# Which DMA engines carry the first 16 KB of wq's rows in a decode block

## The chip, the cores and the metric

The kernel runs on one core of a Trainium2 chip. The core has five compute engines: TensorE (PE, with its weight loads as PEld), VectorE (DVE), ScalarE (ACT), GpSimd (POOL) and SyncE (SP), and sixteen DMA engines, numbered 0 to 15, that move data between device memory and the on-chip buffer. The metric is the time of one execution in microseconds. The kernel before takes 1314.82 us, the median of three runs (1314.66 to 1314.83).

## The reference

One step of a decoding transformer block in float32, for two sequences of one token each. `x` is 2 x 1 x 512, the key and value caches are 2 x 8 x 32768 x 128 (268 MB each), `wq` is 512 x 4096, `wo` 4096 x 512, the three MLP matrices 512 x 1792, 512 x 1792 and 1792 x 512.

```python
def _A_ref(x, k_cache, v_cache, wq, wo):
    q = (x @ wq) as [B, Hq, Sq, Dh]               # 32 query heads of 128
    k, v = k_cache, v_cache, each head repeated 4 times
    p = softmax(q . k * Dh ** -0.5)               # over 32768 cached positions
    return (p . v as [B, Sq, Hq * Dh]) @ wo

def _B_ref(x, W_gate, W_up, W_down):
    gate = x @ W_gate
    gate = gate * (gate > 0)
    return (gate * (x @ W_up)) @ W_down

xn = _layernorm(x)
return x + _A_ref(xn, ...) * silu(_B_ref(xn, ...))
```

Nearly all of the bytes are the caches, and each is read once.

## The kernel before

**Ring.** All large operands pass through a ring of three slots of 128 partitions x 64 KB (`ring`, `slot`). The first three tiles are `wq`, then the two up-projections of the MLP side by side (`gu`), then the down-projection (`wd`). After them come the caches in groups: for each of the 16 pairs of sequence and key head, two K tiles and two V tiles of 8 MB (`load_k`, `load_v`), and last `wo` in six pieces (`WO_PIECES`). A slot is taken again when the last instruction that reads it is done; so the load of a K or V tile waits on SP, at `L72` (`load`), for the engine that frees the slot three tiles back. The instructions of each engine stand in the order in which the code is written; no scheduler moves them.

**A tile's load.** `wq` is viewed as 128 rows of 64 KB, one to a partition: row p holds matrix rows 4p to 4p+3, 16 KB each. A load over 128 partitions is split evenly over the sixteen DMA engines, eight rows each.

**The moved part of wq.** The first 6 KB of each of the 128 rows (`SHIFT = 1536` values) is left out of the large load and is fetched by loads of its own into a spare part of the third slot (`moved`): six of 20 rows, written with the source as five by four rows, one of five rows and one of three. They stand on SP behind the large `wq` load, with the gate matrix between the fifth and the sixth.

**The projection.** `project_q` multiplies the normalised x (`xnp`, transposed to partitions) with the large part of `wq`, then with the moved rows (`xnx` holds the x values that belong to them, zero where the spare part has no row), all into the same accumulators. The result is turned into `qz`, which the scores use. The MLP (`mlp_gu`, `mlp_h`, `mlp_down`) follows.

**A group.** K is transposed in place by DVE (`turn`, `L355`, the costliest group of instructions), PE forms the scores (`score`, `L369`), ACT the exponentials (`L412`), PE the sum over V (`values`, `L436`). The K tile's slot is free after its scores, the V tile's after its products.

**The end.** The last `wo` piece lands, eight small matmuls (`L536`), two DVE operations (`L566`, `L567`) and the store (`L570`) follow.

Of the kernel before, what the change touches and what calls it, by code (L numbers as in the profile page):

```python
# [13 lines left out]
P = 128  # L14
# [8 lines left out]
SHIFT = 1536  # L23
SPREAD = 5
# [5 lines left out]
def kernel(  # L30
# [37 lines left out]
    def slot(name):  # L68
        return ring.tile([P, SLOT], F32, tag="r", align_bytes=ALIGN, name=name)

    def load(dst, src):
        nc.sync.dma_start(dst, src)  # L72

    wqs, gus, wds = slot("wq"), slot("gu"), slot("wd")
    QN = wq.shape[1]
    HP = P // 2
    SET = 4 * SPREAD
    FULL = P // SET
    REST = [(FULL * SET, SPREAD), (FULL * SET + SPREAD, P - FULL * SET - SPREAD)]
    NT = FULL // 2 + 1  # L80
    load(wqs[:, : SLOT - SHIFT], wq.rearrange("(p i) n -> p (i n)", p=P)[:, SHIFT:])
    moved = wds[:HP, FI * D : FI * D + NT * SHIFT].rearrange("p (t n) -> p t n", t=NT)

# [7 lines left out]
    nc.gpsimd.memset(moved, 0.0)
# [7 lines left out]

    first_rows = wq.rearrange("(p i) n -> p i n", i=NKC)[:, 0, :SHIFT]  # L100

    def place_of(k):
        return slice(Q * (k % 2), Q * (k % 2) + SET), k // 2

    for k in range(FULL + len(REST)):
        if k == 5:
            load_gu(0, wg)
        part, t = place_of(k)
        if k < FULL:
            rows = first_rows[k * SET : (k + 1) * SET, :]  # L110
            load(moved[part, t, :], rows.rearrange("(b a) n -> a b n", b=4))
        else:
            at, n = REST[k - FULL]
            dst = moved[part, t, :].rearrange("(a b) n -> a b n", b=4)[:n, 0, :]
            load(dst, first_rows[at : at + n, :])
# [7 lines left out]
    nc.gpsimd.memset(eps_t, EPS)  # L123
    HQR = Q // NS
# [17 lines left out]
    nc.vector.memset(o_ps, 0.0)  # L142

# [13 lines left out]
    xnx = const.tile([HP, NT, 32], F32, name="xnx")  # L157
    nc.vector.memset(sq, 0.0)
    xfirst = xc.rearrange("m (p i) -> m i p", i=NKC)[:, 0, :]
    for k in range(FULL + len(REST)):  # L160
        to = sq[:, k * Q : k * Q + SET].rearrange("m (a b) -> m a b", b=4)
        if k < FULL:
            cols = xfirst[:, k * SET : (k + 1) * SET]
            nc.vector.tensor_copy(to, cols.rearrange("m (b a) -> m a b", b=4))
        else:
            at, n = REST[k - FULL]
            nc.vector.tensor_copy(to[:, :n, 0], xfirst[:, at : at + n])
# [3 lines left out]
    for t in range(NT):  # L171
        nc.tensor.transpose(
            m_ps[:HP, (NKC + t) * 32 : (NKC + t + 1) * 32],
            sq[:, t * HP : (t + 1) * HP],
            ident[:32, :32],
        )
    nc.vector.tensor_copy(xnp.rearrange("p k m -> p (k m)"), m_ps[:, : NKC * 32])
    nc.vector.tensor_copy(
        xnx.rearrange("p k m -> p (k m)"), m_ps[:HP, NKC * 32 : (NKC + NT) * 32]
    )  # L180

    spread = work.tile([P, 4, 4, Q], F32, tag="row", name="spread", bufs=3)
    for kb in range(4):
        nc.gpsimd.tensor_copy(
            spread[:, :, kb, :], ident.rearrange("p (e l) -> p e l", e=4)
        )
# [35 lines left out]
    def project_q():  # L222
        pick = ident.rearrange("p (c m) -> p c m", c=4)[:, :, :B]
        nq = 2 * REP * 4 * B
        def products(half, part):
            pq = S[0][:, half]
            for k in part:
                for c in range(4):
                    n0 = (half * 4 + c) * 512
                    cut = min(512, max(0, SHIFT - n0))  # L230
                    last = NKC + NT - 1 if cut else NKC - 1
                    i = NKC - 1 - k
                    at = cut if i == 0 else 0
                    if k < NKC and at < 512:
                        lo = i * QN + n0 - SHIFT
                        lhs, rhs, a, b = xnp[:, i, :], wqs[:, lo + at : lo + 512], at, 512
                    elif k >= NKC and cut:
                        t = k - NKC
                        lhs, rhs, a, b = xnx[:, t, :], moved[:, t, n0 : n0 + cut], 0, cut
                    else:  # L240
                        continue
                    nc.tensor.matmul(  # L242
                        pq[32 * c : 32 * c + 32, a:b],
                        lhs,
                        rhs,
                        start=(k == 0),
                        stop=(k == last),
                    )
# [219 lines left out]
    project_q()  # L468
    mlp_gu(0)
    mlp_gu(1)  # L470
    ht = mlp_h()
    mlp_down(ht)

    def load_k(g, u):
        KT[g * NU + u] = load_tile(kc, g * NU + u, f"k_{g}_{u}")
# [128 lines left out]
```

## Time and profile before

| | |
|---|---|
| median of the runs | 1314.82 us |
| the profiled execution's own time | 1314.66 us |
| its span, first to last instruction | 1312.9 us |
| around the span | 1.76 us |
| PE busy | 689.7 us (53%) |
| DVE busy | 638.3 us (49%) |
| ACT, POOL busy | 27.6 us, 11.0 us |
| read from device memory | 564.67 MB, 430 GB/s over the span |
| mean granted TensorE clock | 0.746 |

The times of the page are those of one profiled execution. PE and DVE are each busy half of the time. The row "DMA" in the page's forty slices stands at 9, which means 90% or more, in all but the last slice. A view that gives the busy time of each engine by stretches of the span has at its end the DMA engines' busy share and the rate in GB/s; a share of 1.00 is sixteen engines at work all the time. The list of DMA queues names the packets that come from the kernel's loads (`hardware_dynamic`) and those that fetch instructions (`instruction`).

### The profile page before, as it was taken

Reading aid. Unit: us, or ns where it says so; the run is one execution under the profiler, and the core shown is the slowest. Engines: PE = TensorE matmul, PEld = TensorE weight load, DVE = VectorE, ACT = ScalarE, POOL = GpSimd, SP = SyncE. Lnnn points to the kernel's source line nnn. Section 1 sums busy time; section 2 is a strip of 40 time slices with the busy share of each in tenths; the row PEclk is TensorE's granted clock in tenths of the full one; section 3 lists DMA queues with packets and bytes.
Section 4 is the critical chain, followed back from the end, with each engine's and each line's share of the span. In section 5 each row is a group of like instructions: output and inputs, shape, how many; then the busy total and the mean of one; then the engine's idle time right before and its main releaser. Section 6 shows DMA issues by size and latency. Waiting matters only on the chain.

```text
span 1312.9 us, 9882 instructions
## 1 busy us (share of the span) xinstructions
PE 689.7 (53%) x4614; PEld 184.4 (14%) x4614; DVE 638.3 (49%) x244; ACT 27.6 (2%) x69; POOL 11.0 (1%) x24
## 2 busy tenths in 40 slices
PE   3626266372635637264563726556272654825476
PEld 1201011010111101010120101111010111201121
DVE  2273461916447191653709255281835628178510
ACT  0000000000000000000000000000000000000000
POOL 3000000000000000000000000000000000000000
PEclk9757687785777777677786667877676777867878
DMA  9999999999999999999999999999999999999998
GB/s 406 440 431 438 438 429 430 437 424 443 434 430 438 430 432 438 433 434 436 426 438 432 438 433 434 427 441 424 439 438 428 438 432 430 438 435 428 440 422 342
DMA packets 11059, 565.30 MB, mean 431 GB/s; under 512 B 1281, under 2 KB 1289, under 8 KB 1803
## 3 DMA queue, kind: packets, MB, share of 16 engines
q1 hardware_dynamic: 10974, 564.67, 99.4%
q8 instruction: 36, 0.59, 0.2%
q14 instruction: 5, 0.03, 0.0%
q10 hardware_dynamic: 44, 0.01, 0.0%
HBM read 564.67 MB, written 0.00 MB: 430 GB/s over the span
## 4 chain that ended last, share of the span: by engine, by line
DMA 49%; DVE 25%; PE 24%; issue 1%; ACT 1%; DVEq 0%; ACTq 0%
DMA k<-in_A_k_cache_dram 40%; DVE k L355 21%; PE o_ps L436 10%; PE s L369 7%; PE pt_ps L415 4%; DMA v<-in_A_v_cache_dram 3%; DMA wo<-in_A_wo_dram 3%; DVE pt L419 2%; DMA wq<-in_A_wq_dram 2%; DVE m L379 1%; DMA wd<-in_A_wq_dram 1%; PE m_ps L423 1%; PE s L290 1%; ACT w L412 1%; PE m_ps L404 0%
## 5 line engine op out<-in xcount | busy, mean ns | idle before, releaser
L355 DVE STREAM_TRANSPOSE k<-k 128x8192 f32<-128x8192 f32 (+2 forms) x52 | 553.3, 10666 | 176.4 <-DMA k<-in_A_k_cache_dram 176.4
L369 PE MATMUL s<-k,qz 128*32 128x512 f32 x2048 | 299.1, 742 | 496.5 <-DVE k L355 496.5
L436 PE MATMUL o_ps<-v,pt 128*16 128x512 f32 x2048 | 257.0, 665 | 6.8 <-DMA v<-in_A_v_cache_dram 6.8
L369 PEld LDWEIGHTS s<-k,qz 128*32 128x32 f32 x2048 | 71.0, 132 | 718.8 <-DVE k L355 536.0
L448 DVE SCALAR_TENSOR_TENSOR os<-o_ps,rl,mask 128x512 f32<-128x512 f32 x16 | 12.0, 751 | 252.4 <-PE o_ps L436 252.4
L436 PEld LDWEIGHTS o_ps<-v,pt 128*16 128x16 f32 x2048 | 58.6, 105 | 191.2 <-issue 182.4
L415 PE MATMUL pt_ps<-w,perm 128*128 128x512 f32 x64 | 57.6, 997 | 34.5 <-ACT w L412 17.9
L379 DVE TENSOR_REDUCE m<-s 128x1 f32<-128x1024 f32 x16 | 19.6, 1225 | 89.5 <-PE s L369 89.5
L419 DVE STREAM_TRANSPOSE pt<-pt_ps 128x512 f32<-128x512 f32 x32 | 22.9, 715 | 71.6 <-PE pt_ps L415 71.6
L412 ACT ACTIVATE w<-s,nb 128x512 f32<-128x512 f32 x32 | 21.7, 683 | 1178.6 <-DVE nb L408 1178.6
L415 PEld LDWEIGHTS pt_ps<-w,perm 128*128 128x128 f32 x64 | 14.2, 277 | 54.1 <-issue 36.0
L460 PE MATMUL ot_ps<-os,place 128*128 128x256 f32 x64 | 16.0, 392 | 7.1 <-DVE os L448 7.1
L423 PE MATMUL m_ps<-l,same 128*128 128x1 f32 x32 | 9.4, 362 | 13.5 <-DVE l L422 13.5
L395 PE MATMUL m_ps<-ident,m 128*1 128x128 f32 x16 | 4.3, 270 | 20.4 <-DVE m L379 20.4
L460 PEld LDWEIGHTS ot_ps<-os,place 128*128 128x128 f32 x64 | 11.5, 189 | 15.7 <-DVE os L448 14.4
L423 PEld LDWEIGHTS m_ps<-l,same 128*128 128x128 f32 x32 | 8.0, 311 | 38.7 <-DVE l L422 38.7
L404 PE MATMUL m_ps<-negs,mrow 1*128 1x1 f32 x32 | 6.3, 263 | 10.4 <-DVE mrow L403 10.4
L242 PE MATMUL s<-wq,xnp 128*32 128x512 f32 x58 | 9.0, 739 | 4.5 <-DMA wq<-in_A_wq_dram 4.5
L255 DVE COPY qs<-s 128x512 f32<-128x512 f32 x2 | 1.3, 687 | 19.8 <-PE s L242 19.8
L290 PE MATMUL s<-gu,xnp 128*32 128x448 f32 x64 | 8.6, 692 | 0.8 <-DVE gu L298 0.8
L170 PE MATMUL m_ps<-ident,xc 32*128 32x32 f32 x4 | 0.7, 300 | 14.8 <-DVE xc L155 14.8
L427 DVE RECIPROCAL rl<-m_ps 128x1 f32<-128x1 f32 x16 | 2.7, 169 | 10.8 <-PE m_ps L423 10.8
(78 smaller groups left out, 95.7 us busy)
## 6 DMA issues: line engine op xcount, KB each, us to landing
v<-in_A_v_cache_dram SPq DMA_DIRECT2D x2, 4096.0 KB
wq<-in_A_wq_dram SPq DMA_DIRECT2D x1, 7424.0 KB
wo<-in_A_wo_dram SPq DMA_DIRECT2D x1, 4096.0 KB
gu<-in_B_W_gate_dram SPq DMA_DIRECT2D x1, 3584.0 KB
gu<-in_B_W_up_dram SPq DMA_DIRECT2D x1, 3584.0 KB
wd<-in_B_W_down_dram SPq DMA_DIRECT2D x1, 3584.0 KB
wo<-in_A_wo_dram SPq DMA_DIRECT2D x1, 2048.0 KB
wo<-in_A_wo_dram SPq DMA_DIRECT2D x1, 1024.0 KB
```

The source lines that it names most:

```text
L242: nc.tensor.matmul(pq[32 * c : 32 * c + 32, a:b], lhs, rhs, start=(k == 0), stop=(k == last),)
L290: nc.tensor.matmul(ps[32 * c : 32 * c + 32, :FC], xnp[:, i, :], gut[:, w, i, c * FC : (c + 1) * FC], start=(i == 0), stop=(i == NKC - 1),)
L355: nc.vector.transpose(KT[t][:, part], KT[t][:, part])
L369: nc.tensor.matmul(S[g % 2][Q * c : Q * c + Q, u], qz[:, lo : lo + Q], mov[:, s, c, e], start=(s == 0 and e == 0), stop=(s == NS - 1 and e ...
L379: nc.vector.tensor_reduce(MX[g], S[g % 2], axis=AX.XY, op=ALU.max)
L412: nc.scalar.activation(w, S[g % 2][:, u], AF.Exp, bias=nb, scale=SCALE, accum_out=LS[g][:, u : u + 1])
L415: nc.tensor.matmul(pt_ps, perm, w, start=True, stop=True)
L419: nc.vector.transpose(pt.rearrange("p j m -> p (j m)"), pt_ps)
L423: nc.tensor.matmul(m_ps[:, 300:301], same.rearrange("p r h -> p (r h)"), l, start=True, stop=True)
L436: nc.tensor.matmul(o_ps[Q * a : Q * a + NC * REP], w[:, j, s * NC * REP : (s + 1) * NC * REP], v[:, s, j], start=(u == 0 and s == 0 and j ...
L448: nc.vector.scalar_tensor_tensor(OS[hk][:, b], o_ps, RL.pop(g), mask.unsqueeze(2).to_broadcast([P, NC, DH]), op0=ALU.mult, op1=ALU.mult,)
L460: nc.tensor.matmul(ot_ps.rearrange("p b c i -> p (b c) i"), place[:, lo : lo + P], src[:, dq], start=(hk == 0 and dq == 0), stop=(hk == HK ...
```

## The change

1. `wq` is split elsewhere. Of 80 of the 128 rows, rows 0 to 79, the first 16 KB (one whole matrix row) are left out of the large load; the other 48 rows are loaded whole. The large part is now two loads: 80 rows of 48 KB and 48 rows of 64 KB. Each spreads evenly over sixteen engines, five rows and three rows to an engine.
2. 56 of the 80 pieces of 16 KB are fetched on SP by four loads: 20 rows and 20 rows (five engines, four rows each), 10 rows (five engines, two each) and 6 rows (three engines, two each).
3. The other 24 pieces are fetched by one load that GpSimd issues, as two by twelve rows, which the words of the change give to engines 7 and 8. Ahead of it GpSimd issues a tiny load of seven rows of 32 bytes into a tile that nothing reads (`aside`); the words of the change are that it steps over seven engines.
4. The part of `wq`'s slot that the 80 pieces would have filled is set to zero by GpSimd, so that the products run over the whole slot; the products are all 512 columns wide, 32 of them over the slot and 16 over the moved rows, where there were 29 and 12.
5. The order at the start is turned round: gate, up and down matrices are loaded first, the MLP is computed first, and `wq` comes last. The first K tile is loaded in two halves. Its first half is transposed ahead of the second part of `project_q`.

The bytes that each engine carries of `wq`, in KB, worked out from the shapes of the loads, with the engines that the words of the change name:

| engines | before | after | difference |
|---|---|---|---|
| 0, 1, 2 | 464 + 156 = 620 | 432 + 192 = 624 | +4 |
| 3, 4 | 464 + 150 = 614 | 432 + 160 = 592 | -22 |
| 7, 8 | 464 | 432 + 192 = 624 | +160 |
| 5, 6, 9 to 15 | 464 | 432 | -32 |

The order of the instructions shows three places. The first is SP at the start of the program, whose rows are the loads of the three slots and of the first tiles of the caches. Before:

```order
L72 DMA wq<-in_A_wq_dram 128x14848
L72 DMA wd<-in_A_wq_dram 20x1x1536 x5
L72 DMA gu<-in_B_W_gate_dram 128x7168
L72 DMA wd<-in_A_wq_dram 20x1x1536
L72 DMA wd<-in_A_wq_dram 5x1536
L72 DMA wd<-in_A_wq_dram 3x1536
L72 DMA gu<-in_B_W_up_dram 128x7168
L72 DMA wd<-in_B_W_down_dram 128x7168
L72 DMA k_0_296<-in_A_k_cache_dram 128x16384
L72 DMA k_1_298<-in_A_k_cache_dram 128x16384
```

The same place of the changed kernel:

```order
L72 DMA gu<-in_B_W_gate_dram 128x7168
L72 DMA gu<-in_B_W_up_dram 128x7168
L72 DMA wd<-in_B_W_down_dram 128x7168
L72 DMA wd<-in_A_wq_dram 20x1x4096 x2
L72 DMA wd<-in_A_wq_dram 10x1x4096
L72 DMA wd<-in_A_wq_dram 6x1x4096
L72 DMA wq<-in_A_wq_dram 80x12288
L72 DMA wq<-in_A_wq_dram 48x16384
L72 DMA k_0_253<-in_A_k_cache_dram 128x8192 x2
L72 DMA k_1_304<-in_A_k_cache_dram 128x16384
```

The large part of `wq` went from the first place to the last before the caches, the moved rows stand ahead of it, and the first K tile now takes the slot of `gu`, the second that of `wq`.

The second place is GpSimd near its start, in the changed kernel (`aside` is the tile that nothing reads, `wd` the third slot with its spare part):

```order
L87 MEMSET wd 128x4096
masks.py:197 MEMSET ident 128x128
masks.py:199 ISA
masks.py:199 AFFINE_SELECT ident<-ident 128x128
L116 MEMSET eps_t 32x1
L120 DMA aside<-in_A_x_dram 7x2x4
L102 DMA wd<-in_A_wq_dram 24x1x4096
L125 MEMSET wq 80x4096
L128 MEMSET qz 128x2064
```

Between `eps_t` and `qz` there was nothing before; the two loads and the clearing of `wq`'s slot are new there.

The third place is DVE between the MLP and the first scores, in the changed kernel (`qs`, `turned` and `qz` are the steps that turn the projection into what the scores use):

```order
L318 COPY down<-m_ps 128x512
L349 STREAM_TRANSPOSE k_0_253<-k_0_253 128x8192
L249 COPY qs_278<-s_108 128x512
L249 COPY qs_284<-s_108 128x512
L260 COPY turned<-m_ps 128x64
L273 COPY qz<-pt_ps 32x32x4 x8
```

Before, the copies of `qs`, `turned` and `qz` stood ahead of the MLP's operations, and the whole K tile was transposed in one instruction behind `down`; now half a K tile is transposed between them.

The diff, with the parts left out that only rename:

```diff
-SHIFT = 1536
-SPREAD = 5
+MOVES = ((5, 4, 0, 0), (5, 4, 32, 0), (5, 2, 0, 1), (3, 2, 32, 1), (2, 12, 52, 0))
+UNDER = 7
...
-    load(wqs[:, : SLOT - SHIFT], wq.rearrange("(p i) n -> p (i n)", p=P)[:, SHIFT:])
-    moved = wds[:HP, FI * D : FI * D + NT * SHIFT].rearrange("p (t n) -> p t n", t=NT)
+    OUT = firsts[-1]
+    moved = wds[:, FI * D : FI * D + NT * QN].rearrange("p (t n) -> p t n", t=NT)
...
-    nc.gpsimd.memset(moved, 0.0)
+    nc.gpsimd.memset(moved[:, 0], 0.0)
+    nc.vector.memset(moved[:, 1:], 0.0)
...
-    for k in range(FULL + len(REST)):
-        if k == 5:
-            load_gu(0, wg)
-        part, t = place_of(k)
-        if k < FULL:
-            rows = first_rows[k * SET : (k + 1) * SET, :]
-            load(moved[part, t, :], rows.rearrange("(b a) n -> a b n", b=4))
...
+    def move(k, start):
+        a, b, lo, t = MOVES[k]
+        rows = wqrows[firsts[k] : firsts[k + 1], :QN].rearrange("(b a) n -> a b n", b=b)
+        start(moved[lo : lo + a * b, t, :], rows)
+
+    load_gu(0, wg)
     load_gu(1, wu)
     load(wds[:, : FI * D], wd.rearrange("(p i) d -> p (i d)", p=P))
+    for k in range(len(MOVES) - 1):
+        move(k, load)
+    load(wqs[:OUT, QN:], wqrows[:OUT, QN:])
+    load(wqs[OUT:, :], wqrows[OUT:, :])
...
+    view = x[0, 0, : UNDER * 32].rearrange("(p w) -> p w", p=UNDER)[:, :16]
+    nc.gpsimd.dma_start(
+        aside[:UNDER].rearrange("p (u n) -> p u n", u=2),
+        view.rearrange("p (u n) -> p u n", u=2)[:, :, :4],
+    )
+    move(len(MOVES) - 1, nc.gpsimd.dma_start)
+    nc.gpsimd.memset(wqs[:OUT, :QN], 0.0)
...
-        for part in (range(NKC), range(NKC, NKC + NT)):
-            for half in range(2):
-                products(half, part)
+        for half in range(2):
+            products(half, range(NKC))
+        yield
+        spread = work.tile([P, 4, 4, Q], F32, tag="row", name="spread", bufs=3)
...
+        for half in range(2):
+            products(half, range(NKC, NKC + NT))
...
-    project_q()
-    mlp_gu(0)
-    mlp_gu(1)
-    ht = mlp_h()
-    mlp_down(ht)
...
+    mlp_gu(0)
+    mlp_gu(1)
+    mlp_down(mlp_h())
+    steps = project_q()
+    next(steps)
+    load_k(0, 0, NS)
+    turn(0, 0)
+    for _ in steps:
+        pass
+
     for g in range(NG - 2):
-        for u in range(NU):
+        for u in range(1 if g == 0 else 0, NU):
             load_k(g, u)
```

More of the change, by code (lines that the diff above doesn't have):

```diff
@@ L72, in load @@
         nc.sync.dma_start(dst, src)
-    wqs, gus, wds = slot("wq"), slot("gu"), slot("wd")
+    gus, wqs, wds = slot("gu"), slot("wq"), slot("wd")
     QN = wq.shape[1]
[L76 to L80, printed above, removed]
-    load(wqs[:, : SLOT - SHIFT], wq.rearrange("(p i) n -> p (i n)", p=P)[:, SHIFT:])
-    moved = wds[:HP, FI * D : FI * D + NT * SHIFT].rearrange("p (t n) -> p t n", t=NT)
+    NT = 1 + max(t for *_, t in MOVES)
+    firsts = [sum(a * b for a, b, *_ in MOVES[:k]) for k in range(len(MOVES) + 1)]
+    OUT = firsts[-1]
+    moved = wds[:, FI * D : FI * D + NT * QN].rearrange("p (t n) -> p t n", t=NT)
     row = work.tile([P, 512], F32, tag="row", name="xp", bufs=3)
@@ L98, in load_gu @@
         )
-    first_rows = wq.rearrange("(p i) n -> p i n", i=NKC)[:, 0, :SHIFT]
-    def place_of(k):
-        return slice(Q * (k % 2), Q * (k % 2) + SET), k // 2
-    for k in range(FULL + len(REST)):
-        if k == 5:
-            load_gu(0, wg)
-        part, t = place_of(k)
-        if k < FULL:
-            rows = first_rows[k * SET : (k + 1) * SET, :]
-            load(moved[part, t, :], rows.rearrange("(b a) n -> a b n", b=4))
[L112 to L115, printed above, removed]
+    wqrows = wq.rearrange("(p i) n -> p (i n)", p=P)
+    def move(k, start):
[3 more added lines that the diff above has]
+    load_gu(0, wg)
     load_gu(1, wu)
     load(wds[:, : FI * D], wd.rearrange("(p i) d -> p (i d)", p=P))
+    for k in range(len(MOVES) - 1):
+        move(k, load)
+    load(wqs[:OUT, QN:], wqrows[:OUT, QN:])
+    load(wqs[OUT:, :], wqrows[OUT:, :])
     wdt = wds[:, : FI * D].rearrange("p (i d) -> p i d", i=FI)
@@ L123 @@
     nc.gpsimd.memset(eps_t, EPS)
+    aside = const.tile([P, 8], F32, name="aside")
+    view = x[0, 0, : UNDER * 32].rearrange("(p w) -> p w", p=UNDER)[:, :16]
[5 more added lines that the diff above has]
+    nc.gpsimd.memset(wqs[:OUT, :QN], 0.0)
     HQR = Q // NS
@@ L142 @@
     nc.vector.memset(o_ps, 0.0)
+    nc.vector.memset(xy, 0.0)
     st = const.tile([32, 8], F32, name="st")
@@ L156 @@
     xnp = const.tile([P, NKC, 32], F32, name="xnp")
-    xnx = const.tile([HP, NT, 32], F32, name="xnx")
+    xnx = const.tile([P, NT, 32], F32, name="xnx")
     nc.vector.memset(sq, 0.0)
     xfirst = xc.rearrange("m (p i) -> m i p", i=NKC)[:, 0, :]
[L160 to L167, printed above, removed]
+    sqt = sq[:, : NT * P].rearrange("m (t p) -> m t p", t=NT)
+    for k, (a, b, lo, t) in enumerate(MOVES):
+        nc.vector.tensor_copy(
+            sqt[:, t, lo : lo + a * b].rearrange("m (a b) -> m a b", b=b),
+            xfirst[:, firsts[k] : firsts[k + 1]].rearrange("m (b a) -> m a b", b=b),
+        )
     xcol = xc.rearrange("b (p i) -> b i p", i=NKC)
@@ L172 @@
         nc.tensor.transpose(
-            m_ps[:HP, (NKC + t) * 32 : (NKC + t + 1) * 32],
-            sq[:, t * HP : (t + 1) * HP],
+            m_ps[:, (NKC + t) * 32 : (NKC + t + 1) * 32],
+            sqt[:, t, :],
             ident[:32, :32],
@@ L178 @@
     nc.vector.tensor_copy(
-        xnx.rearrange("p k m -> p (k m)"), m_ps[:HP, NKC * 32 : (NKC + NT) * 32]
+        xnx.rearrange("p k m -> p (k m)"), m_ps[:, NKC * 32 : (NKC + NT) * 32]
     )
[L182 to L186, printed above, removed]
     same = const.tile([P, Q, REP], F32, name="same")
@@ L229, in products @@
                     n0 = (half * 4 + c) * 512
[L230 to L239, printed above, removed]
+                    if k < NKC:
+                        lhs, rhs = xnp[:, k, :], wqs[:, k * QN + n0 : k * QN + n0 + 512]
                     else:
-                        continue
+                        lhs, rhs = xnx[:, k - NKC, :], moved[:, k - NKC, n0 : n0 + 512]
                     nc.tensor.matmul(
-                        pq[32 * c : 32 * c + 32, a:b],
+                        pq[32 * c : 32 * c + 32],
                         lhs,
@@ L246, in products @@
                         start=(k == 0),
-                        stop=(k == last),
+                        stop=(k == NKC + NT - 1),
                     )
-        for part in (range(NKC), range(NKC, NKC + NT)):
-            for half in range(2):
-                products(half, part)
+        for half in range(2):
+            products(half, range(NKC))
+        yield
+        spread = work.tile([P, 4, 4, Q], F32, tag="row", name="spread", bufs=3)
+        for kb in range(4):
+            nc.gpsimd.tensor_copy(
+                spread[:, :, kb, :], ident.rearrange("p (e l) -> p e l", e=4)
+            )
+        for half in range(2):
+            products(half, range(NKC, NKC + NT))
         for half in range(2):
@@ L466, in finish_group, with load_k @@
                 )
-    project_q()
-    mlp_gu(0)
-    mlp_gu(1)
-    ht = mlp_h()
-    mlp_down(ht)
-    def load_k(g, u):
-        KT[g * NU + u] = load_tile(kc, g * NU + u, f"k_{g}_{u}")
+    def load_k(g, u, pieces=1):
+        KT[g * NU + u] = load_tile(kc, g * NU + u, f"k_{g}_{u}", pieces)
     def load_v(g, u, pieces=1):
```

1 line of the change is left out of this document (removed).

## The prediction

> **What bounds the kernel now.** I read the busy shares first, then the DMA queues, then the end of the span in short windows, then the start in the chain of waits and the timeline. The compute engines have room (DVE, the busier in the middle, is at half), so the first question is whether the DMA engines ever stand still. These are windows of the span; the last two columns are the DMA engines' busy share and GB/s.
>
> ```profile
> 300.00:700.00 400.00, 203.27 (x1349) 53.56 (x1349) 204.08 (x61) 7.24 (x20) 0.00 (x0) 0.73 1.00 434
> 700.00:1260.00 560.00, 299.17 (x1999) 77.95 (x2003) 296.88 (x91) 10.13 (x28) 0.00 (x0) 0.74 1.00 434
> ...
> 1301.00:1302.00 1.00, 1.00 (x16) 0.25 (x12) 0.00 (x0) 0.00 (x0) 0.00 (x0) 1.00 0.96 408
> 1301.90:1306.90 5.00, 3.56 (x36) 0.63 (x32) 0.00 (x0) 0.00 (x0) 0.00 (x0) 1.00 0.78 321
> 1307.00:1307.50 0.50, 0.50 (x8) 0.00 (x0) 0.00 (x0) 0.00 (x0) 0.00 (x0) 1.00 0.77 303
> 1307.50:1308.00 0.50, 0.31 (x4) 0.00 (x0) 0.12 (x1) 0.00 (x0) 0.00 (x0) 1.00 0.47 180
> 1308.00:1308.50 0.50, 0.50 (x16) 0.32 (x16) 0.50 (x1) 0.00 (x0) 0.00 (x0) 1.00 0.35 135
> 1308.50:1309.00 0.50, 0.50 (x22) 0.32 (x16) 0.07 (x1) 0.00 (x0) 0.00 (x0) 1.00 0.12 45
> ```
>
> Through 960 us all sixteen engines work without a gap, at 434 GB/s together, 27.1 GB/s each. So one engine needs 0.60 us for 16 KB and 1.21 us for 32 KB. The kernel is bound by the DMA engines, and strictly by the one that finishes last. The end shows how unevenly they finish. Up to 1302 nearly all work; from there 0.78 of sixteen, so three of them (at most three and a half) are done about 7 us before the rest. The other thirteen drop out between 1307.4 and 1308.9. After that only a fixed tail is left, which the chain of waits shows:
>
> ```profile
> 1270.44 38.81 DMA wo<-in_A_wo_dram
> 1309.29 0.44 PE s L536 x8
> 1309.75 0.30 DVE res L566
> ```
>
> Why three are early follows from the queues and the loads. The columns of the queues are packets, MB, and share of sixteen engines' span.
>
> ```profile
> q1 hardware_dynamic: 10974, 564.67, 99.4%
> q8 instruction: 36, 0.59, 0.2%
> ...
> wq<-in_A_wq_dram SPq DMA_DIRECT2D x1, 7424.0 KB
> gu<-in_B_W_gate_dram SPq DMA_DIRECT2D x1, 3584.0 KB
> wd<-in_A_wq_dram SPq DMA_DIRECT2D x6, 120.0 KB
> wd<-in_A_wq_dram SPq DMA_DIRECT2D x1, 30.0 KB
> wd<-in_A_wq_dram SPq DMA_DIRECT2D x1, 18.0 KB
> ```
>
> The moved rows put 150 to 156 KB on five engines that the other eleven don't have: 5.7 to 5.9 us. If nothing else differed, those five would end that much after eleven others. Instead three are early and thirteen are together, so eight of the eleven lose about 6 us to something else. The instruction packets fit: 0.2% of 16 x 1312.9 us is 42 us (31 to 53 by the rounding), 5.3 us on each of eight engines. So my reading is five engines (0 to 4) with extra rows, eight with the instruction packets, three with neither. The profile doesn't say which three of 5 to 15 these are.
>
> **The change part by part.** *Bytes.* By the loads' shapes engines 0 to 2 get 4 KB more than before (+0.15 us), 3 and 4 get 22 KB less (-0.83), the engines without moved rows 32 KB less (-1.21), and 7 and 8, if they are the ones, 160 KB more (+6.04).
>
> If 7 and 8 are two of the early three, they end at 1301.9 + 6.0 = 1307.9 instead of 1301.9. The eight with the instruction packets end 1.2 earlier, at 1307.7 at the latest. The five then set the end. Their last one is somewhere between 1307.4 and 1308.9 now, and moves by -0.83 to +0.15. So the end of the last load is between 1307.9 (where the pair stands) and 1309.05, against 1308.9: -1.0 to +0.15 us. I take the middle, rounded: **-0.5 us**. Nothing but the five holds it back: the eight have 1.2 us of new room.
>
> An upper limit on any gain stands in the same windows. The idle engine time from 1301.9 to 1308.9 is (0.22 x 5.0 + 0.23 x 0.6 + 0.53 x 0.5 + 0.65 x 0.5 + 0.88 x 0.4) x 16, about 35 us, or 2.2 us on each of sixteen. No better sharing of the same bytes saves more.
>
> *The start.* Everything that is new there stands ahead of or beside the queues' work, which must not run dry. The rows it rests on:
>
> ```profile
> 0.73 20.02 DMA wq<-in_A_wq_dram
> 20.78 13.68 DMA wd<-in_A_wq_dram
> ...
> 44.35 5.37 PE s L290 x32
> ...
> 50.42 3.26 PE s L290 x32
> ...
> 0.73 5.21 POOL L91 MEMSET wd<- 64x6144 f32 x1 [0.29 <-POOLq L584]
> 0.90 0.48 DVE L86 MEMSET xp<- 32x512 f32 x1 [0.90 <-PEq L584]
> 9.55 0.67 DVE L148 TENSOR_REDUCE st<-xp 32x1 f32<-32x512 f32 x1 [7.44 <-DMA xp<-in_A_x_dram]
> 20.89 9.00 PE L242 MATMUL s<-wq,xnp 128*32 128x512 f32 x58 [4.52 <-DMA wq<-in_A_wq_dram]
> 21.72 0.23 PEld L242 LDWEIGHTS s<-wq,xnp 128*32 128x32 f32 x4 [0.62 <-issue]
> 22.57 0.23 PEld L242 LDWEIGHTS s<-wq,xnp 128*32 128x32 f32 x4 [0.62 <-issue]
> 25.41 0.14 PEld L242 LDWEIGHTS s<-wq,xnp 128*32 128x32 f32 x4 [0.29 <-issue]
> 25.84 0.14 PEld L242 LDWEIGHTS s<-wq,xnp 128*32 128x32 f32 x4 [0.29 <-issue]
> 29.92 24.11 SPq L72 DMA_DIRECT2D k<-in_A_k_cache_dram  x2
> 37.68 1.29 DVE L255 COPY qs<-s 128x512 f32<-128x512 f32 x2 [19.82 <-PE s L242]
> 44.39 2.39 DVE L279 COPY qz<-pt_ps 32x128 f32<-32x128 f32 x8 [2.12 <-PE pt_ps L268]
> 71.31 17.25 DVE L355 STREAM_TRANSPOSE k<-k 128x16384 f32<-128x16384 f32 x1 [10.32 <-DMA k<-in_A_k_cache_dram]
> 88.61 9.27 PE L369 MATMUL s<-k,qz 128*32 128x512 f32 x64 [27.14 <-DVE k L355]
> ```
>
> The first load carried 464 KB per engine, 17.5 us of bytes, and took 20.0: 2.5 us of start and landing. The moved rows landed at 34.46, which fits five engines: 464 + 150 + 6 KB and one matrix of 224 KB make 844 KB, 31.9 us, plus 0.7 and 2.5, is 35; spread over sixteen they would have landed by 31.
>
> The clearings are cheap: 6144 columns took POOL 5.21 us, so 4096 take 3.5, twice; DVE's 512 columns took 0.48, so 4096 take 3.8. DVE waited 7.44 us for x there, which hides it. POOL's new load instructions appear nowhere in this trace. From below they cost nothing, from above as much as POOL's longest row, 5.2 us each. Behind them stand the clearing of `wq`'s slot, `qz` and `place`; DVE waits for `place` ahead of the MLP's copies, and even with 10 us of loads that is cleared by 0.7 + 3.5 + 0.6 + 10 + 3.5 + 2.2 = 21 us, ahead of the first product to be copied. I take no time on the path.
>
> The first K tile waits for the MLP's first two products, and these for two matrices of 224 KB (16.9 us of bytes and 3.2 of start make 20, up to 7 more on engines 7 and 8, whose moved rows share the way) and 5.4 and 3.3 us of products. It is issued by about 36 us, with 41.7 us of bytes (672 + 432 KB) queued on the lightest engine. That is safe.
>
> The second K tile is the tight place. It takes `wq`'s slot, and `wq` now lands last: 672 + 624 KB is 49.0 us, plus 0.7 and 2.5, is 52.2. Then 64 product rows follow; 58 took 9.0 us, so 64 take 9.9, and the load is issued at 62. A light engine, with 1104 KB and 512 KB of the first K tile, ends its queue at 0.7 + 2.5 + 41.7 + 19.3 = 64.2. So some 2 us are left for a load to be issued and to begin, and a light engine may stand dry for nothing or for a few tenths; the eight have 0.5 us more room than the five at the end (1.2 against 0.5 to 0.7), which covers that.
>
> DVE now transposes half a K tile before `qs`. The half lands at about 52.2 + 9.7 = 62, takes 8.6 (half of 17.25), then the way from `qs` to `qz` took 37.68 to 46.78, 9.1 us: `qz` is ready at 80. The second half is transposed from 80 to 88.5. Before, the whole tile was done at 88.56 and the first scores started at 88.61. So the steady part starts as it did, and the order behind it is unchanged.
>
> **Sum.** -0.5 us at the end of the loads, nothing at the start, the tail of 4 us as it is: 1314.66 - 0.5 = 1314.2 for the profiled execution. The median of the runs is 0.16 above that execution, so **1314.3 us**. A measurement of this kernel can tell about 0.2%, 2.6 us, from no change.
>
> The page "DMA: Bandwidth & Descriptors" of the Trainium skill, section "Latency and other measured facts", says that engines 7 and 15 are usually slower and guesses that descriptors written for GpSimd loads cause it; this change puts the very first GpSimd load on 7. No trace here has such a load, so no row tells; before, no single engine stood out by more than the early three. Its result is the third rival.
>
> **The rivals.**
>
> *The wrong engines (0.16).* 7 or 8 are among the eight with the instruction packets, or the step of seven doesn't take place and the 24 rows fall on other engines. For it: the profile names no early engine, and three of eleven is few. Against it: only that the reading needs just these two. The price is decided by one packet row: an engine of the eight ends between 1307.4 and 1308.9 and gets 6.04 us more, so 1313.4 to 1314.9, 4.5 to 6.0 us later than now. Falling on 0 and 1 (192 KB, 7.25 us, on top of +0.15) it is up to 7.4. That is 1319.3 to 1322.2, **slower**. It decides as soon as one of the two engines has no 6 us to spare. The Trainium skill, page "DMA: Bandwidth & Descriptors", section "Why a DMA increments its semaphore by 16 and not by 1", speaks of a cursor that goes round the engines and of GpSimd loads that are spread over all sixteen regardless; by the latter the seven-row load would not move it.
>
> *The queue runs dry at 63 us (0.08).* PE has been idle before the products; the rows at 21.72 and 22.57 are 0.85 us apart, those at 25.41 and 25.84 0.43. If all 64 rows go at the slow pace they take 16 x 0.85 = 13.6 us, the load is issued at 66, and the nine lighter engines stand still for 2 to 3.5 us. Less the 1.2 saved, the eight end 0.8 to 2.3 later: up to 1317.1, within the 0.2%. For it: `wq` last and PE cold. Against it: before, only the first five of fifteen groups were slow.
>
> *GpSimd's packets are slow (0.05).* An instruction packet took 42 us / 36 = 1.17 us for 16 KB where a load needs 0.60. If the twelve rows on each of 7 and 8 go at that pace, these two lose 12 x 0.57 = 6.8 us more and end at 1314.7, 5.8 late: 1320.6, **slower**. The Trainium skill's rule on engine 7, named above, would come out on this side too.
>
> **How the numbers follow.** The forecast has 0.68, of which all is within 0.2%. The dry queue adds 0.08 there. The two slower rivals have 0.21. The rest, 0.03, is a gain that I can't place, since 2.2 us is the most that the end holds. So faster 0.03, same 0.76, slower 0.21. The likeliest case alone ranges from 1313.2 to 1315.4 (-1.0 and +0.15, widened by half a microsecond for the start). The whole range goes from 1312.8, 2.0 us down, about the limit that the end sets, to 1319.6, which takes in the dry queue and the first of the wrong-engine cases and leaves out some 0.18 above.
>
> **What would show it.** Right: in the last 12 us the share stays near 1.00 to about 1307 but for one engine's part (0.93), and falls to zero by 1308.5; the second K load is issued at 60 to 62; the first scores end no later than before. Wrong: a share of 0.12 or 0.06 over 5 us at the end (one or two engines alone, the wrong ones), a window below 0.9 near 63 us (the dry queue), or DVE waiting for the first K tile beyond 72.

## The result, and the profile after

The changed kernel takes 1351.91 us (median of five runs, 1351.41 to 1354.63) where the kernel before takes 1314.82 (1314.66 to 1314.94): the ratio of the runs is 1.0286, 95% interval 1.0275 to 1.0297. It is 37 us slower. The profiled execution has a span of 1349.7 us, 36.8 more than before, and an own time of 1351.43.

Where the time went stands in the page's forty slices, 33.7 us each. This is the GB/s row of the changed kernel.

```profile
GB/s 347 208 277 422 432 436 436 436 436 434 433 432 435 430 432 436 434 436 436 436 432 435 434 428 435 430 435 434 436 434 434 432 434 434 430 435 434 434 429 328
```

Nearly all is lost in the first three slices. From the fifth slice on the rate is what it was. Windows of the first 110 us, with the same columns as in the prediction (the last two are the busy share of the DMA engines and GB/s), first of the changed kernel:

```profile
0.00:10.00 10.00, 0.00 (x0) 0.00 (x0) 7.14 (x7) 0.00 (x0) 9.39 (x12) 1.00 0.85 336
10.00:17.40 7.40, 1.07 (x6) 0.83 (x6) 4.99 (x12) 2.86 (x3) 1.60 (x3) 1.00 1.02 425
17.40:30.00 12.60, 5.71 (x32) 1.40 (x33) 1.89 (x7) 0.00 (x0) 1.61 (x9) 0.85 1.01 338
30.00:84.00 54.00, 11.24 (x68) 2.98 (x68) 3.41 (x5) 1.56 (x2) 0.99 (x4) 0.59 1.01 204
84.00:110.00 26.00, 13.65 (x102) 4.62 (x102) 9.88 (x3) 0.00 (x0) 0.00 (x0) 0.76 0.92 377
...
700.00:1260.00 560.00, 296.67 (x1987) 78.38 (x1991) 290.04 (x92) 10.14 (x28) 0.00 (x0) 0.74 1.00 434
```

and of the kernel before:

```profile
17.40:30.00 12.60, 9.11 (x61) 2.60 (x64) 0.46 (x2) 0.00 (x0) 1.44 (x9) 1.00 1.03 440
30.00:84.00 54.00, 22.97 (x148) 9.34 (x142) 20.53 (x18) 2.84 (x3) 0.00 (x0) 0.70 1.00 434
84.00:110.00 26.00, 14.94 (x108) 3.80 (x112) 21.86 (x3) 0.00 (x0) 0.00 (x0) 0.76 1.01 439
```

From 30 to 84 us the share is 1.01 in the changed kernel and 1.00 in the kernel before, and the rate is 204 GB/s in one and 434 in the other. This is the line to learn from: the DMA engines are not waiting for a load to be issued, each of them has a packet under way all the time, and each packet takes about twice as long. A busy share of 1.00 says that the engines are occupied, not that bytes flow.

The three windows lose 12.6 x (1 - 338/434) + 54 x (1 - 204/434) + 26 x (1 - 377/434) = 2.8 + 28.6 + 3.4 = 34.8 us of full rate. That is nearly all of the 36.8. (In the third window the share is 0.92: part of its 3.4 us is DMA engines that stood idle.) The compute engines follow. The timeline of the changed kernel (start, us busy, engine and line, and in brackets the idle time before and what ended it) and SP's waits (total, times, longest):

```profile
17.60 5.71 PE L284 MATMUL s<-gu,xnp 128*32 128x448 f32 x32 [0.38 <-DVE xnp L178]
30.01 4.64 PE L284 MATMUL s<-gu,xnp 128*32 128x448 f32 x32 [6.69 <-DMA gu<-in_B_W_up_dram]
55.07 6.17 PE L310 MATMUL m_ps<-wd,ht 128*32 128x512 f32 x28 [20.43 <-DMA wd<-in_B_W_down_dram]
90.19 9.12 PE L229 MATMUL s<-wq,xnp 128*32 128x512 f32 x64 [27.73 <-DMA wq<-in_A_wq_dram]
99.56 8.71 DVE L349 STREAM_TRANSPOSE k<-k 128x8192 f32<-128x8192 f32 x1 [37.59 <-DMA k<-in_A_k_cache_dram]
116.18 6.34 PE L363 MATMUL s<-k,qz 128*32 128x512 f32 x32 [1.35 <-DVE qz L273]
...
SPq L72 <- DMA wq<-in_A_wq_dram: 34.8, 1, 34.8
```

`wq` landed at 90.2 us, 38 us after the 52.2 of the prediction, and the first scores started at 116.2 instead of 88.6.

The trace also has a record of every packet: its start, its size and how long it took, but not its engine. These are the packets of one size that start together, in the order of their start. The times are what most packets of the group took, with the fastest and the slowest tenth left out (in the kernel before, most packets take 1.06 us for 28 KB, 1.21 for 32 KB, 2.19 for 58 KB and 2.42 for 64 KB):

```
changed kernel                       start     us of one packet    at 27.1 GB/s
mostly gate, up    28 KB rows        3..17     1.06 to 1.08        1.06
mostly down        28 KB rows       17..31     1.1 to 1.65         1.06
the last 14        28 KB rows       32..51     2.2 to 3.1          1.06
moved rows, SP     16 KB rows       31..45     1.2 to 1.3          0.61
wq, 80 rows        48 KB rows       31..70     3.6 to 4.6          1.81
wq, 48 rows        64 KB rows       49..84     4.8 to 5.9          2.42
first K tile       32 KB rows       64..83     2.4 to 2.9          1.21
first K tile       32 KB rows       85..88     1.36                1.21
```

So the first half of the 28 KB rows runs at full speed, the rest is slowed, the two loads of `wq` and the moved rows are at about half speed, and so is the first K tile up to 83 us (the last row of `wq` ends at 88.9).

### The profile page after: what moved, and what is told of

The parts are those of the page before. It is cut to its first block, busy times and chain, and to the rows that moved or that the text cites. A ratio compares the mean times of both kernels' runs of the same rounds, so it can differ in the third digit from the quotient of the medians.

```text
span 1349.7 us, 9903 instructions
## 1 busy us (share of the span) xinstructions
PE 695.9 (52%) x4626; PEld 185.8 (14%) x4626; DVE 644.7 (48%) x243; ACT 27.6 (2%) x69; POOL 13.6 (1%) x27
## 4 chain that ended last, share of the span: by engine, by line
DMA 40%; DVE 21%; PE 20%; issue 6%; ACT 1%; SPq 0%; DVEq 0%; ACTq 0%
DMA k<-in_A_k_cache_dram 37%; DVE k L349 18%; PE o_ps L430 9%; PE s L363 6%; PE pt_ps L409 3%; DMA wo<-in_A_wo_dram 3%; DVE pt L413 1%; DVE m L373 1%; ACT w L406 1%; PE m_ps L417 1%; PE m_ps L398 0%; PE m_ps L389 0%; DVE mr L391 0%; DVE mrow L397 0%; DVE nb L402 0%
## 5 line engine op out<-in xcount | busy, mean ns | idle before, releaser
L363 PE MATMUL s<-k,qz 128*32 128x512 f32 x2048 | 305.3, 755 | 475.6 <-DVE k L349 474.2
L229 PE MATMUL s<-wq,xnp 128*32 128x512 f32 x64 | 9.1, 733 | 27.7 <-DMA wq<-in_A_wq_dram 27.7
L310 PE MATMUL m_ps<-wd,ht 128*32 128x512 f32 x28 | 6.2, 993 | 20.4 <-DMA wd<-in_B_W_down_dram 20.4
```

The lines of the kernel that those rows point to most:

```text
L229: nc.tensor.matmul(pq[32 * c : 32 * c + 32], lhs, rhs, start=(k == 0), stop=(k == NKC + NT - 1),)
L363: nc.tensor.matmul(S[g % 2][Q * c : Q * c + Q, u], qz[:, lo : lo + Q], mov[:, s, c, e], start=(s == 0 and e == 0), stop=(s == NS - 1 and e ...
```

## The experiments

**The theories.** *P, doors.* Bytes enter the on-chip buffer by sixteen doors, each as fast as one DMA engine. Partitions 4c to 4c+3 and the four that lie 32 above them share one. A load over 128 partitions gives each engine the rows of one door; a load of 80, 64 or 48 rows gives each engine neighbouring rows instead, and two or three engines meet at a door. *H, reading.* Groups of five and three rows are slow to read from device memory. *G.* The load that GpSimd issues slows the queues. *O.* The new order, with `wq` last, leaves the queues without work.

P is worked out from the Trainium skill, page "SBUF — State Buffer", section "Door 1: The DMA port swizzle (why `[64,N]` ≈ `[32,N]`)": "DMA bandwidth depends on how many of the 16 SBUF ports your partitions reach." That each engine of a 128-partition load serves one port stands on the Trainium skill's page "DMA: Bandwidth & Descriptors", section "The descriptor swizzle". Whether they hold here is what the next runs tell.

The first six of the kernels below were run once each; the kernel before took 1314.77 to 1314.89 us beside them. The differences to it are 8 us and more. Differences to the changed kernel are taken to its profiled execution, 1351.43 us; its five runs lie 3.2 us apart, so these differences are known to some 3 us only.

### The load of wq cut otherwise, or GpSimd's load left out

```diff
-    load(wqs[:OUT, QN:], wqrows[:OUT, QN:])
-    load(wqs[OUT:, :], wqrows[OUT:, :])
+    load(wqs[:, QN:], wqrows[:, QN:])
+    load(wqs[OUT:, :QN], wqrows[OUT:, :QN])
```

> The changed kernel with the large part of wq cut otherwise: one load of 128 rows of 48 KB and one of 48 rows of 16 KB, instead of 80 rows of 48 KB and 48 rows of 64 KB. Each engine carries the same 432 KB. Theory P (a load whose partitions reach only some of the sixteen doors into the on-chip buffer is slow, whatever engines carry it): the 128-row load takes the 384 KB / 27.1 = 14.2 us of full rate, the 48-row load 128 KB a door = 4.7 us instead of 1.8; about 17 us less than the changed kernel and, since the K halves no longer stand behind a late wq, up to 30 less: 1317 to 1325 us, wq landing at 56 to 62 instead of 90. Theory G (the GpSimd load slows the queues): 1350, no change, since that load is still there. Theory H (the reading side: rows in groups of five and three to an engine): fast, 1316 to 1322. Theory O (the order at the start, wq last, makes the queue run dry): 1345 to 1352.

1329.85 us, 21.6 less than the changed kernel. The same bytes to an engine, in the same order and beside the same GpSimd load, take that much less when most of them go over 128 partitions. G and O alone are out. It is above the 1317 to 1325 of P, so something else was left.

The other part, GpSimd's two loads and nothing else taken out of the changed kernel:

```diff
-    nc.gpsimd.dma_start(
-        aside[:UNDER].rearrange("p (u n) -> p u n", u=2),
-        view.rearrange("p (u n) -> p u n", u=2)[:, :, :4],
-    )
-    move(len(MOVES) - 1, nc.gpsimd.dma_start)
```

> The changed kernel without its two GpSimd loads: the 24 moved rows' share of the projection is left out. Theory P: the loads of 80 and 48 rows are slow by themselves; what goes away is what the GpSimd rows took from the loads beside them between 11 and 37 us (some 5 us of the down matrix and a few tenths of us around): 1344 to 1349. Theory G: the loss is gone, 1314 to 1316. Theory H: 1344 to 1349. Theory O: 1350 or so.

1344.91 us, 6.5 less than the changed kernel. Windows of this kernel:

```profile
10.00:28.00 18.00, 9.32 (x70) 3.00 (x70) 8.13 (x22) 2.86 (x3) 2.18 (x11) 1.00 1.02 433
28.00:64.00 36.00, 5.75 (x36) 1.70 (x36) 0.80 (x2) 1.56 (x2) 0.99 (x4) 0.58 1.03 209
64.00:80.00 16.00, 0.00 (x0) 0.00 (x0) 0.00 (x0) 0.00 (x0) 0.00 (x0) 0.50 0.98 195
```

The stretch to 28 us, in which the up and down matrices come, is whole again, 433 GB/s where the changed kernel had 338 from 17.4 to 30 us. The stretch behind it is as slow as ever. So the cut of `wq` makes the slow stretch from 28 us on by itself, and GpSimd's rows make what is lost before it and, with 6.5 us against 2.8 in that window, something behind it: in the changed kernel the last rows of the down matrix were still under way at 53 us, when `wq` had long begun. Whether a GpSimd load costs anything by itself is open at this point.

### The kernel before with its own load cut

Three edits of one statement, each of the kernel before and of nothing else:

```diff
-    load(wqs[:, : SLOT - SHIFT], wq.rearrange("(p i) n -> p (i n)", p=P)[:, SHIFT:])
+    wqr = wq.rearrange("(p i) n -> p (i n)", p=P)
+    load(wqs[:80, : SLOT - SHIFT], wqr[:80, SHIFT:])
+    load(wqs[80:, : SLOT - SHIFT], wqr[80:, SHIFT:])
```

> The kernel before with one edit: its large wq load is split in two, 80 rows and 48 rows of the same 58 KB; no byte, order or GpSimd load is changed otherwise. Full rate is 464 KB an engine, 17.1 us. Theory P: 80 rows reach 8 doors with 8 rows each, 464 KB a door = 17.1 us; 48 rows reach 4 doors with 8 rows... of 58 KB + 0 = 464 KB a door each = 17.1 us: 34 us instead of 17, so wq lands at about 37 instead of 20.8 and the kernel takes 1330 to 1333. Theory H (reading in groups of five and three rows): slow too, of the same order. Theories G and O: 1314.8, nothing of theirs is in it.

```diff
+    load(wqs[:64, : SLOT - SHIFT], wqr[:64, SHIFT:])
+    load(wqs[64:, : SLOT - SHIFT], wqr[64:, SHIFT:])
```

> The kernel before with its large wq load split in two of 64 rows. Theory P: 64 rows reach 8 doors with 8 rows each, so 464 KB a door twice, 34 us instead of 17: 1330 to 1333, the same as the split into 80 and 48. Theory H (odd groups of rows on the reading side): groups of four, so less than with 80 and 48: 1315 to 1325. Theories G and O: 1314.8.

```diff
+    for lo, hi in ((32, 96), (0, 32), (96, 128)):
+        load(wqs[lo:hi, : SLOT - SHIFT], wqr[lo:hi, SHIFT:])
```

> The kernel before with its large wq load cut into three: partitions 32 to 95 (64 rows) first, then 0 to 31 and 96 to 127 (32 rows each), rows of 58 KB. Theory P (a door belongs to four neighbouring partitions and the four that lie 32 above; two engines that write to one door share its 27 GB/s): a 64-row load gives each engine four neighbouring rows; from partition 32 on these are sixteen different doors, so its rows take 2.2 us, as in the kernel before, though 64 rows from partition 0 took 4.65. The two loads of 32 rows give each engine two rows, two engines to a door: 4.4 to 4.65 us each. In all 4 x 2.2 + 4 x 4.5 = 27 us instead of 17.5: 1324 to 1325. Theory H (the reading side, which is the same rows in the same groups as in the split into 64 and 64): all rows at 4.65, 1334 or more.

They took 1341.86, 1334.11 and 1324.82 us, against 1314.8. The packet records give the reason, row by row (58 KB each; each engine's first packet in the program is left out, since its time differed from the rest):

```
                       us of one packet    engines at one door, at most
128 rows (before)      2.19 to 2.3         1
rows 0..79             4.4 to 4.9          2
rows 80..127           6.5 to 7.65         3
rows 0..63             4.65                2
rows 64..127           4.5 to 4.65         2
rows 32..95            2.19                1
rows 0..31, 96..127    4.0 to 4.65         2
```

The last column is worked out, from P's map and from the shapes of the loads: with five neighbouring rows to an engine, engine 0 begins at partition 0 and engine 7 at 35, one door; with three from 80 on, engines 0, 1 and 11 begin at 80, 83 and 113, again one door. It gives the size of the duration in every row, 2.19 times one, two or three (6.6 for three, where 6.5 to 7.65 were measured).

In the loads of 64 and 32 rows the map has every engine share its door with one other or none. In the loads of 80 and 48 rows it doesn't: in the second row of each engine, six of sixteen stand alone at their door in the 80-row load and two in the 48-row load. Yet all sixteen packets took 4.50 to 4.55 us there, and 7.31 to 7.65. So all engines of such a load go at the pace of the slowest ones. Why they do is not shown by these runs.

Windows of the kernel cut into 64 and 64, and of the one that begins at 32, show the same as rates:

```profile
4.00:38.00 34.00, 1.44 (x8) 1.04 (x8) 6.00 (x22) 1.58 (x2) 7.49 (x20) 1.00 0.95 196
```

```profile
5.00:11.00 6.00, 0.00 (x0) 0.00 (x0) 2.64 (x5) 0.26 (x1) 4.89 (x11) 1.00 1.03 446
```

The two 64-row loads that stand here read rows in the same groups of four with the same spacing, and write them to partitions 0 to 63 and 32 to 95. One runs at 4.65 us a row and the other at 2.19. That speaks against H, by which both would be equally slow. The rows read are 32 further on as well, so the pair does not settle it alone; the run with GpSimd's rows at other engines' doors, below, changes nothing but the partitions that are written. The Trainium skill's section on Door 1, named above, gives about 218 GB/s for partitions 0 to 63; sixteen rows of 58 KB in 4.65 us are 204.

My price for the 80 and 48 cut, 1330 to 1333, was too low, and for the 64 and 64 cut by a little (1334.11). For 80 and 48 I had counted the bytes at the fullest door, not that all engines of a load go at the pace of those that meet. (By the map partitions 80 to 127 reach eight doors, not the four that I wrote.) The first products with `wq`, in the 80 and 48 cut and in the 64 and 64 cut:

```profile
48.56 9.27 PE L244 MATMUL s<-wq,xnp 128*32 128x512 f32 x58 [25.84 <-DMA wq<-in_A_wq_dram]
```

```profile
40.21 10.02 PE L244 MATMUL s<-wq,xnp 128*32 128x512 f32 x58 [21.12 <-DMA wq<-in_A_wq_dram]
```

The delay of `wq` passes to the end whole, or nearly: its products started at 48.6 us instead of 20.9 in the 80 and 48 cut, 27.7 later, and the kernel took 27.1 more; 40.2 in the 64 and 64 cut, 19.3 later, and 19.3 more.

### What is left, and the same idea without meetings

The first two edits together, to see whether they add:

> The changed kernel with both edits: the large part of wq as 128 rows of 48 KB and 48 rows of 16 KB, and without the GpSimd loads (the share of their 24 rows in the projection is left out). What is still out of line with the doors are the 48 rows of 16 KB, three to an engine, and the small loads of 10 and 6 rows. If the costs of the two edits add up: 1351.4 - 21.6 - 6.5 = 1323.3 us. By theory P alone, without any effect of late rows on the loads behind them: 8 rows of 16 KB at one door, 4.8 us instead of 1.8, and a little for the small loads, 1318 to 1320. Theory O: some 1320 or more is left whatever the cut, but the kernel with all loads in line took 1315.3 in the same order, so that a time above that is due to these small loads.

1322.73 us, so they add to within 0.6 us, closer than the runs of the changed kernel lie together. 8 us are left over the kernel before, more than the 3 to 5 of P's byte count. The packets show where: the 32 KB rows of the first K tile mostly take 2.0 to 2.5 us between 52 and 58 us, while rows of the 48-row load (0.9 to 1.9 us instead of 0.61) are still under way. The K rows themselves go over 128 partitions; by P's map, engines that are late with their rows of `wq` meet other engines' K rows at the doors.

Then the kernel in which every row goes to a door of its engine's own: `wq` as 128 rows of 48 KB and, for the first 16 KB, the 64 rows of partitions 32 to 95, the other 64 pieces in blocks of four neighbouring partitions.

```diff
-MOVES = ((5, 4, 0, 0), (5, 4, 32, 0), (5, 2, 0, 1), (3, 2, 32, 1), (2, 12, 52, 0))
+MOVES = ((4, 4, 0, 0, 0), (5, 4, 32, 0, 96), (3, 4, 0, 1, 116))
+POOLED, PLACE = 16, 60
...
-    load(wqs[:OUT, QN:], wqrows[:OUT, QN:])
-    load(wqs[OUT:, :], wqrows[OUT:, :])
+    load(wqs[:, QN:], wqrows[:, QN:])
+    load(wqs[Q : 3 * Q, :QN], wqrows[Q : 3 * Q, :QN])
...
+    step(UNDER)
+    pooled(0)
+    step(16 - 2)
+    pooled(1)
```

`step(n)` is the small GpSimd load of n rows, `pooled(t)` one of 8 rows, four to an engine, to partitions `PLACE` and on. Without the four GpSimd loads:

> The changed kernel's order and idea with loads in which each engine writes to a door of its own: 128 rows of 48 KB, then 64 rows (partitions 32 to 95) of 16 KB, and 48 of the other 64 pieces by three loads on engines 0 to 4, four neighbouring partitions to an engine. The last 16 pieces are left out, with their share of the projection, and no GpSimd load is there. Theory P: nothing is left that is slow, rows of 48 KB at 1.81 us and wq at about 50; the end is that of the kernel before by the bytes (engines 0 to 2 carry 624 KB instead of 620, the others 16 KB less): 1314 to 1316. Theory O (wq last makes the queue run dry even so): 1318 to 1323.

With them:

> The same with the 16 pieces loaded by GpSimd, eight to each of engines 7 and 8 and into these engines' own doors (partitions 60 to 67, in two loads, each behind a small one that moves the cursor to 7). Against the kernel without them: if 7 and 8 are two of the engines that are free at the end, 0 to 0.7 us more, 1314 to 1316.5, and at the end one early engine instead of three. If they are among those with instruction packets, 3.5 to 4.2 us more. If a GpSimd load is slow by itself (theory G), 4 to 7 us more, with long rows beside it from 11 us on, as in the changed kernel.

1315.34 (1315.09 to 1315.63, eight runs) and 1315.30 us (1315.13 to 1315.68, eight runs), against 1314.89 (1314.75 to 1315.08); the ratio of each is 1.0003, interval 0.9992 to 1.0014. (The fullest engines carry 640 KB of `wq` here, not the 624 of the expectation.) The 37 us are gone, with `wq` last, GpSimd's load and the cursor's step all in place. Two rows of the timeline and three windows of the kernel with GpSimd's loads:

```profile
53.23 9.11 PE L246 MATMUL s<-wq,xnp 128*32 128x512 f32 x64 [13.14 <-DMA wq<-in_A_wq_dram]
79.50 6.19 PE L380 MATMUL s<-k,qz 128*32 128x512 f32 x32 [1.35 <-DVE qz L290]
...
28.00:64.00 36.00, 16.41 (x120) 4.76 (x124) 4.37 (x6) 1.56 (x2) 0.98 (x4) 0.72 1.01 434
1302.00:1305.00 3.00, 2.71 (x28) 0.48 (x20) 0.00 (x0) 0.00 (x0) 0.00 (x0) 1.00 0.91 381
1305.00:1308.00 3.00, 2.37 (x24) 0.42 (x24) 0.00 (x0) 0.00 (x0) 0.00 (x0) 1.00 0.75 299
```

and the same two windows of the end without GpSimd's loads, then the first of them in the kernel before:

```profile
1302.00:1305.00 3.00, 1.93 (x20) 0.32 (x12) 0.00 (x0) 0.00 (x0) 0.00 (x0) 1.00 0.80 330
1305.00:1308.00 3.00, 2.38 (x24) 0.42 (x24) 0.00 (x0) 0.00 (x0) 0.00 (x0) 1.00 0.71 289
```

```profile
1302.00:1305.00 3.00, 2.10 (x24) 0.38 (x20) 0.00 (x0) 0.00 (x0) 0.00 (x0) 1.00 0.77 320
```

With GpSimd's rows the share of 1302 to 1305 goes from 0.80 to 0.91, by 0.11 or two engines of sixteen (0.125), and the end does not move. So two of the three early engines carry the 16 rows, and do so in time that was free. Engines 7 and 8 are the ones that the step of seven is meant to reach, and the doors the rows were laid out for are, by the map, theirs. All 16 rows took 0.61 us each, which they would not at a door of another engine, as the next run shows. No record names the engines; that they are 7 and 8 rests on these two things.

### GpSimd's rows at other engines' doors

```diff
-POOLED, PLACE = 16, 60
+POOLED, PLACE = 16, 52
```

> The same, but the 16 pieces go to partitions 52 to 59, which by theory P are the doors of engines 5 and 6, with 64 KB at a time. Theory P: the pieces meet the loads of engines 5 and 6 there, 16 KB rows of 1.2 us and more instead of 0.6 and long 28 KB rows beside them, on four engines: 2 to 5 us more than with the pieces in their own doors. Theory G: no difference between the two.

1320.25 us (1319.04 to 1320.67, four runs), 5.0 more than with the pieces in partitions 60 to 67. Against the kernel before the ratio is 1.0037, interval 1.0018 to 1.0057. One constant differs, eight partitions lower; the bytes read, the order and the loads are the same. Its windows:

```profile
10.00:32.00 22.00, 8.44 (x54) 2.91 (x58) 7.04 (x16) 2.86 (x3) 11.79 (x16) 0.90 1.02 362
32.00:64.00 32.00, 17.50 (x104) 4.66 (x100) 3.41 (x5) 1.56 (x2) 0.98 (x4) 0.64 1.00 430
```

and one of the kernel with the pieces at 60 to 67:

```profile
10.00:28.00 18.00, 10.40 (x70) 3.35 (x70) 6.96 (x17) 2.86 (x3) 11.86 (x16) 1.00 1.00 428
```

While GpSimd's rows are under way the rate falls to 362, 22 x (1 - 362/434) = 3.6 us of the 5.0; behind that it is nearly whole. Most of GpSimd's rows take 0.8 to 1.4 us, the 28 KB rows beside them up to 2.3; with the pieces at 60 to 67 they took 0.61 and 1.06. The changed kernel lost time in the same stretch, and its 24 rows lay at partitions 52 to 75, of which by the map 52 to 59 and 68 to 75 are not at the doors of engines 7 and 8. These GpSimd loads cost nothing that can be measured by themselves; G is out, and so is H for these rows, which were read alike in both kernels.

### The pieces shared more evenly

With every row at its own door, what is left of the idea can be had: the 48 pieces of engines 0 to 4 as 10, 10, 10, 10 and 8.

```diff
-MOVES = ((4, 4, 0, 0, 0), (5, 4, 32, 0, 96), (3, 4, 0, 1, 116))
-POOLED, PLACE = 16, 60
+MOVES = ((5, 4, 0, 0, 0), (5, 4, 32, 0, 96), (4, 1, 0, 1, 20), (4, 1, 32, 1, 116))
+POOLED, PLACE = (24, 120), 60
```

> The kernel with every piece in its engine's own door, with the 48 pieces of engines 0 to 4 shared more evenly: 10 each on engines 0 to 3 and 8 on engine 4, instead of 12, 12, 12, 8 and 4. Each of 0 to 3 now carries 448 + 160 = 608 KB of wq, where the kernel before has 620 on its fullest engine and the uneven one 640; the eight with instruction packets carry 448 instead of 464. Theory P with the reading of the end in the prediction: the fullest engines end 0.4 to 0.6 us earlier than in the kernel before, 1314.2 to 1314.6 us; that is 0.03%, below what can be told. A time over 1316 would say that the order at the start costs something that the door alignment hides.

1314.78 us (1314.66 to 1314.92, eleven runs) against 1314.84 (1314.57 to 1315.24, fifteen runs), ratio 0.9999, interval 0.9990 to 1.0009. Its last windows:

```profile
1305.00:1308.00 3.00, 2.22 (x28) 0.35 (x24) 0.28 (x1) 0.00 (x0) 0.00 (x0) 1.00 0.69 272
1308.00:1309.00 1.00, 0.97 (x32) 0.46 (x24) 0.42 (x1) 0.00 (x0) 0.00 (x0) 1.00 0.13 49
```

In the last microsecond the share is 0.13 where the uneven kernel has 0.41 and the kernel before 0.24: the engines end a few tenths earlier. The time is just above the 1314.2 to 1314.6 of the expectation and can't be told from the kernel before.

## Why the prediction was wrong, step by step

**What bounds the kernel: right.** The steady windows stand at 434 GB/s in both kernels, and a microsecond that a load lands late at the start comes out at the end, or nearly (27.7 and 27.1, 19.3 and 19.3).

**Three engines early, eight with instruction packets: right as far as tested.** The pair that GpSimd's rows were put on was early: 0.80 to 0.91 of sixteen engines at the end, and no later end. Which engine is the third is not known, and that the eight are late because of instruction packets is not shown by a run.

**The bytes: too small to tell.** -0.5 us was forecast for the end of the loads, with 624 KB on the fullest engines. That share was not run without meetings at doors. With the same idea and other shares the runs gave +0.4 us (640 KB) and -0.06 (608 KB), and both intervals take in no change at all.

**The start: this is the step that failed.** The prediction wrote "`wq` now lands last: 672 + 624 KB is 49.0 us, plus 0.7 and 2.5, is 52.2", and took no time on the path for the start. The sum has one hidden term: that an engine moves every row at 27.1 GB/s, wherever the row goes. All large loads in the trace of before cover 128 partitions, and the 27.1 came from those. The change replaced one of them by loads of 80 and 48 rows, which no row of that trace showed, and I priced them as if the shape didn't matter. The stretch in which they came ran at 204 GB/s instead of 434, and `wq` landed at 90.2 us instead of 52.2. The rest of the working of this step was sound: GpSimd's two load instructions took 0.71 and 0.60 us, where up to 5.2 each were allowed for, and with each row at its own door `wq` landed at 53.2 us and the first scores started at 79.5, earlier than before.

Split by the runs, the 36.6 us between the changed kernel's profiled time (1351.4) and the 1314.8 of before are, undone one after the other, 21.6 for the large part of `wq` laid over 80 and 48 partitions, 7.1 for GpSimd's rows in partitions 52 to 75 (6.5 if they are undone first), and 7.9 that were left. Of these, 7.4 went with the 48 rows of 16 KB and the small loads, and 0.4 us is left with all three laid out otherwise, or nothing. The first two are known to some 3 us.

The rule that speaks against the change stood in the Trainium skill all along, page "SBUF — State Buffer", in the section on Door 1; I weighed two rules of the DMA page and none of that one. By its map of ports the 80 rows have 8 x 48 KB at the fullest door and the 48 rows 8 x 64 KB; one load after the other these are 896 KB or 34 us at 27.1 GB/s where I counted 432 KB, 16 us: an estimate of 17.5 us more from that page, about half of what the change cost. The trace agrees on the rate at two engines to a door (204 GB/s), and shows more than the count of bytes where three engines meet (6.5 to 7.65 us a packet).

**The rivals.** *The wrong engines* (0.16): fell, with the tail of the kernel with its rows in line. Its price would have been 4.5 to 7.4 us. *The queue runs dry* (0.08): the second K load was issued late in the changed kernel, but because `wq` came late; with the rows in line the same order cost nothing. *GpSimd's packets are slow* (0.05): fell. They took 0.61 us at their own doors; the 5 to 7 us that they cost elsewhere happen to be near the price I gave, by another mechanism. The rule on engine 7 of the Trainium skill, page "DMA: Bandwidth & Descriptors", section "Latency and other measured facts", has nothing to show here: the rows that GpSimd put on the pair took the time of a row on any engine. The Trainium skill's rule on the cursor (same page, section "Why a DMA increments its semaphore by 16 and not by 1") agrees with the two filled engines (0.80 to 0.91).

**The range.** It went to 1319.6 and the result is 32 us above. All of its bounds, below and above, were made of byte counts at one rate and of small stalls; the rate of a load shape that the trace doesn't show was not among the unknown costs, though the step said of GpSimd's loads that they "appear nowhere in this trace". The 80- and 48-row loads were just as new.

## What to carry to other kernels

A load of fewer than 128 partitions can take two or three times as long on each engine, with the same bytes on each (4.5 and 7.4 us a row here, instead of 2.19); before a 128-row load is cut, look at which partitions each engine writes, and cut by columns, or at 32 to 95, rather than by rows from 0. Where DMA engines are at a share of 1.00, read the GB/s beside it: here busy engines at half the rate met at the doors. In a prediction, a duration taken from one shape of load is a bound for another, not a price.

## What the hardware showed that I had not expected

Engines that meet at a door slow loads that are not at fault. A GpSimd load of 24 rows of 16 KB, 16 of them by the map at other engines' doors, cost 6.5 us of sixteen engines, though these rows are only 384 KB, 0.9 us at 434 GB/s; 16 rows at other engines' doors cost 5.0. And the engines of one load stay in step, also those that by the map have their door to themselves: the 48 rows of 58 KB took 6.5 to 7.65 us each, three times the time of a row alone and more, so that the load ran at 16 x 58 KB / 7.4 us = 128 GB/s, below the 217 (8 x 27.1) that eight doors would let through.
